# Fifteen short transfers between the q weights and the first K tile of a decode block

## The chip, the cores and the metric

The kernel runs on one core of a Trainium2 chip. The core has five engines that run their own instruction streams: TensorE (PE, matrix products), VectorE (DVE), ScalarE (ACT), GpSimd (POOL) and SyncE (SP). SP computes nothing here; it issues transfers. The transfers themselves are carried out by 16 DMA engines, which fill the on-chip memory (SBUF, 128 partitions) from the device memory (HBM). The metric is the device time of one execution in microseconds. Three executions of the kernel before took 377.62, 377.65 and 378.11 us; the median is 377.65 us.

## The reference, cut to what matters

One decode step of a transformer block for four sequences: layer norm, attention over the last 4096 positions of a cache with 32 query heads and 16 key heads of width 128, output projection, residual, layer norm, a gated feed-forward with ReLU on the gate, residual.

```python
def _A_ref(x, k_cache, v_cache, wq, wo):        # x: (4, 1, 576)
    W = min(4096, max(256, Sk // 4))            # 4096 of 16384 positions
    q = (x @ wq).reshape(B, Sq, Hq, Dh) ...
    k = jnp.repeat(k_cache[:, :, Sk - W:, :], rep, axis=1)
    v = jnp.repeat(v_cache[:, :, Sk - W:, :], rep, axis=1)
    p = _softmax(einsum("bhqd,bhkd->bhqk", q, k) * Dh ** -0.5)
    return einsum("bhqk,bhkd->bhqd", p, v) ... @ wo
def _B_ref(x, W_gate, W_up, W_down):
    gate, up = x @ W_gate, x @ W_up
    return ((gate * (gate > 0)) * up) @ W_down
h  = x + _A_ref(_layernorm(x), A_k_cache, A_v_cache, A_wq, A_wo)
h2 = h + _B_ref(_layernorm(h), B_W_gate, B_W_up, B_W_down)
```

Everything is bfloat16. Nearly all bytes are the K and V windows (16 tiles of 4 MB each) and the five weight matrices, about 160 MB, and each is used once.

## The kernel before, in words

The kernel is written against a small recorder, the class `Prog`. Calls of `P.op` and `P.dma` append one operation to the list of one engine, with the names of the operations that it depends on; `emit` (L71) then writes each list out in that order and puts a semaphore wait ahead of an operation where a dependency lies on another engine or on a transfer. So the order on each engine is the order in which the Python code records, and nothing is moved afterwards. A transfer raises its semaphore by 16 when all of it has landed.

All large transfers are recorded for SP, in one long list near the top of the kernel (L251 to L286). They land in `arena`, a buffer of 81,920 bfloat16 columns: two areas of 8,192 columns (`QWW`) and then a ring of four slots of 16,384 columns (`NSLOT`, `TILE`). `place` (L216) records a transfer into a stretch of `arena` and makes it wait for the last readers of that stretch. `add_kv` (L235) takes the next slot of the ring for a K or V tile: four heads of one sequence, 128 rows of 32 KB, issued at L242. The list begins with

- L251: the last 64 rows of the q weights into `pp` (128 rows of 4 KB),
- L255: the other 512 rows of the q weights into one ring slot (128 rows of 32 KB, 4 MB),
- L242: K tiles 0, 1 and 2 into the other three slots. None of these five waits for anything.
- L242: K tile 3, which takes the slot of the q weights and so waits for the q products (`QMM`, L381 and L34) that read them; then K and V tiles in turn, each waiting for the products that read the tile before it in its slot,
- L266 to L284: the output projection's weights, gate, up, and the down weights in five pieces.

The transfer of `x` (four rows of 1,152 bytes, L337) is issued from ACT, and SP's last transfer writes the output (L710). After it SP waits for its landing (an operation without an instruction, whose wait is made at L110).

What uses the data: PE makes q from the q weights (L381), ACT spreads q into `arena` (L415). For each K tile DVE transposes 32x32 blocks in place (L424) and PE makes the scores (L448 and, with the weights held, `mm_same`, L34). Every four K tiles the softmax of a sequence follows (L453 to L490), and PE multiplies by the V tiles (L509, L34), whose results DVE and ACT select (L519 to L526). The end is the output projection (L617), a layer norm on small tiles (L620 to L647), gate and up (L666), and the down projection (L690, with the last row's weights loaded at L699), copied out at L708 and L709.

Of the kernel before, what the change touches and what calls it, by code (L numbers as in the profile page):

```python
# [9 lines left out]
BF16 = mybir.dt.bfloat16  # L10
# [110 lines left out]
def bass_sequential_preLN__sliding_block_cached__glu_gated_reglu__decode_kernel(  # L121
# [12 lines left out]
    with ExitStack() as es:  # L134
        cnt = [0]

        def sb(name, shape, dt):
            return es.enter_context(nc.sbuf_tensor("sb_" + name, shape, dt))

        P = Prog()  # L140
# [5 lines left out]

        PPW = 6144
        AW = 2 * QWW + NSLOT * TILE
        arena = sb("arena", [128, AW], BF16)
        pp = sb("pp", [128, PPW], BF16)  # L150
        ident_b = sb("ident_b", [128, 128], BF16)
# [64 lines left out]
        def place(name, off, size, reader, make, key=None):  # L216
            deps = []
            for blk in range(off // 64, (off + size) // 64):
                r = owner.get(blk)
                if r is not None and r not in deps:  # L220
                    deps.append(r)
                owner[blk] = reader
            semk = key or "d_" + "_".join(str(v) for v in name)
            P.dma("sync", ("L",) + name, make, semk, deps)
            land[name] = off
# [3 lines left out]
        def ring_slot():  # L229
            s = ring[0] % NSLOT  # L230
            ring[0] += 1
            return s


        def add_kv(kind, g):  # L235
            b, qd = divmod(g, 4)
            s = ring_slot()
            off = slot0 + s * TILE
            cache = A_k_cache if kind == "K" else A_v_cache
            src = cache[b, 4 * qd:4 * qd + 4, SK - WIN:SK, :].rearrange("a (p t) d -> p a (t d)", p=32)  # L240
            place((kind, g), off, TILE, ("QK", g) if kind == "K" else ("PV", g),
                  lambda e: e.dma_start(out=arena[:, off:off + TILE], in_=src), key=f"slot{s}")  # L242


        def main_rows(W):
            return W[0:512, :].rearrange("(p r) n -> p (r n)", r=4)

        def last_rows(W):
# [5 lines left out]
        place(("wq", 0), wq_off, TILE, "QMM",  # L254
              lambda e: e.dma_start(out=arena[:, wq_off:wq_off + TILE], in_=main_rows(A_wq)), key=f"slot{s}")  # L255
        for g in range(NTILE):
            add_kv("K", g)
            if g >= 4:
                add_kv("V", g - 4)
# [3 lines left out]
        for g in range(NTILE - 4, NTILE):  # L263
# [5 lines left out]
        place(("gu", 0, 4), off, F, ("GU", 1, 4), lambda e, off=off: e.dma_start(  # L269
            out=bass.AP(tensor=arena, offset=off, ap=[[2 * AW, 64], [1, F]]), in_=B_W_gate[512:576, :]))  # L270
        P.dma("sync", ("L", "gu", 1, 4), lambda e, off=off: e.dma_start(
            out=bass.AP(tensor=arena, offset=AW + off, ap=[[2 * AW, 64], [1, F]]), in_=B_W_up[512:576, :]), "d_gu_1_4")
        gu_off[(0, 4)] = gu_off[(1, 4)] = off
# [8 lines left out]
        for r0, r1 in zip(WD_ROWS, WD_ROWS[1:]):  # L282
            place(("wd", r0), wd_off + r0 * D, (r1 - r0) * D, ("DOWN", 1),
                  lambda e, r0=r0, r1=r1: e.dma_start(  # L284
                      out=arena[:, wd_off + r0 * D:wd_off + r1 * D],
                      in_=B_W_down.rearrange("(p r) n -> p (r n)", p=128)[:, r0 * D:r1 * D]))  # L286
# [18 lines left out]
                                                in_=c_qm[:, :, :].rearrange("p q (h j) -> p q h j", j=4),  # L305
# [4 lines left out]
                                                in_=to_v[:, :, :].rearrange("p n (k a) -> p n k a", a=4),  # L310
# [14 lines left out]
        for sg in range(2):  # L325
            pool(f"c_toq{sg + 1}", lambda e, sg=sg: e.affine_select(
                out=toq[:, :, :, :], in_=toq[:, :, :, :],
# [84 lines left out]
        def put_q():  # L412
            for i in range(4):
                for q in range(2):
                    act("QW", lambda e, i=i, q=q: e.copy(  # L415
                        out=bass.AP(tensor=arena, offset=32 * i * AW + 2 * i + q, ap=[[AW, 32], [512, 16], [136, 4], [32, 4]]),
                        in_=bass.AP(tensor=q_keep, offset=q, ap=[[512, 32], [32, 16], [8, 4], [2, 4]])),
# [9 lines left out]
        def pe_qk(g):  # L427
            b, qd = divmod(g, 4)
            for cb in range(4):
                for w in range(2):  # L430
                    for a in range(4):
# [8 lines left out]
                        lhsT = arena[:, b * 2048 + cb * 512 + g % 4 * 128 + a * 32:][:, 0:32]  # L440
                        rhs = bass.AP(tensor=arena, offset=off, ap=[[AW, 128], [128, 64], [16, 4], [4, 2]])
                        out_ = bank[w][32 * a:32 * a + 32, :]
# [98 lines left out]
        def finish_o():  # L541
            for q in range(4):
                for qd in range(4):
# [17 lines left out]
                                              in_=bass.AP(tensor=e8, offset=0, ap=[[8, 128], [0, 4], [1, 8]])), ["c_e8", "c_selc0"])  # L561
# [47 lines left out]
        for a in range(8):  # L609
            for n in range(2):  # L610
                for j in range(4):
# [4 lines left out]
                    else:  # L616
# [6 lines left out]
                                             in_=bass.AP(tensor=psb, offset=512 + 224, ap=[[4096, 128], [1, 64], [0, 2]])), ["part1"])  # L623
# [54 lines left out]
        for i in range(2):  # L678
            dve(("HHT", i), lambda e, i=i: e.transpose(
                out=hhT[:, 576 * i:576 * i + 576].rearrange("p (r q) -> p r q", q=32),  # L680
                in_=bass.AP(tensor=pp, offset=3712 + 18 * i, ap=[[PPW, 128], [1, 18], [36, 32]])), [("HH", m) for m in range(3)])
# [26 lines left out]
        dve("OUT0", lambda e: e.tensor_copy(out=out_sb[:, 0:272], in_=bank[0][0:32, 0:272]), [("DOWN", 0)])  # L708
        act("OUT1", lambda e: e.copy(out=out_sb[:, 272:576], in_=bank[1][32:64, 0:304]), [("DOWN", 1)])  # L709
        P.dma("sync", "O", lambda e: e.dma_start(out=out.rearrange("b s d -> (b s) d"), in_=out_sb[0:B, :]), "d_out", ["OUT1", "OUT0"])  # L710
        P.op("sync", None, None, ["O"])
        P.emit(nc, es)


# [26 lines left out]
```

## Time and profile before

| what | value |
|---|---|
| median of three executions | 377.65 us (377.62 to 378.11) |
| the profiled execution | 378.22 us |
| its span, first to last instruction | 377.0 us |
| DMA: bytes, mean rate | 159.74 MB, 424 GB/s |
| share of the 16 DMA engines' time on SP's queue (q1) | 98.7% |
| PE, DVE, ACT busy | 57%, 61%, 14% of the span |
| granted PE clock, mean | 0.796 |

The profile has a page, and views that a reader can ask for: a timeline of instructions, a chain of waits that ended last, sums of waits, and DMA queues. "SPq" stands for SP issuing a transfer: that duration is the issuing only, and the transfer goes on afterwards. "us to landing" runs from the issue to the moment at which the semaphore has its full count. Under the views lie the trace's records of single DMA packets (start, duration, bytes, queue; the number of the DMA engine is not kept) and of single landings: each transfer over 16 DMA engines leaves 16 landings, one for each engine.

### The profile page before, as it was taken

The page shows a single profiled execution, that of the slowest core. Times are in us where ns is not written, and L with a number is a line of the kernel's source. Part 1 is how long each engine was busy: PE and PEld are TensorE (multiplying, and loading weights), DVE is VectorE, ACT ScalarE, POOL GpSimd, SP SyncE. Part 2 cuts the span into 40 slices and gives each one's busy share as a digit, 9 for nine tenths or more (in the row PEclk, how much of TensorE's full clock was granted, in tenths as well). Part 3 has the DMA queues.
Part 4 walks back from the last instruction along what each step waited for, and adds up shares of the span by engine and source line. Part 5 has one row for each costly group of instructions (what it writes and reads, how often), then busy time and mean ns, then how long its engine had stood idle before and what let it go on. Part 6 is the DMA issues. An engine that isn't in the chain of part 4 may idle for free.

```text
span 377.0 us, 2556 instructions
## 1 busy us (share of the span) xinstructions
PE 213.8 (57%) x1462; PEld 39.9 (11%) x694; DVE 228.8 (61%) x164; ACT 53.7 (14%) x84; POOL 10.5 (3%) x29
## 2 busy tenths in 40 slices
PE   0404443239919091749282844664655787886658
PEld 0000000001001010001010100110000101002316
DVE  4088878779292969584847778665749433333240
ACT  3093000211000114010101140101010411112010
POOL 8200000000000000000000000000000000000000
PEclk9966666659969788696877786989695968998686
DMA  8999999999999999999999999999999999999996
GB/s 334 445 445 428 405 445 442 396 442 445 398 435 445 442 433 403 442 445 435 407 436 445 435 414 431 441 438 431 417 442 438 426 417 442 418 433 437 427 414 256
DMA packets 6378, 159.74 MB, mean 424 GB/s; under 512 B 728, under 2 KB 864, under 8 KB 1248
## 3 DMA queue, kind: packets, MB, share of 16 engines
q1 hardware_dynamic: 6360, 159.59, 98.7%
q8 instruction: 8, 0.13, 0.1%
q14 instruction: 2, 0.02, 0.0%
q10 hardware_dynamic: 8, 0.00, 0.0%
HBM read 159.58 MB, written 0.00 MB: 423 GB/s over the span
## 4 chain that ended last, share of the span: by engine, by line
DMA 60%; PE 20%; DVE 18%; SPq 1%; issue 0%; ACT 0%
DMA sb_arena<-in_A_k_cache_dram 53%; DVE sb_arena L424 16%; PE psb L34 11%; DMA sb_arena<-in_B_W_down_dram 7%; PE psb L448 4%; PE psb L509 3%; PE psb L690 2%; DVE sb_o_tmp L522 1%; DVE sb_pp L487 1%; SPq L242 0%; PE psb L475 0%; SPq L255 0%; ACT sb_out_sb L709 0%; SPq L251 0%; DVE sb_f L534 0%
## 5 line engine op out<-in xcount | busy, mean ns | idle before, releaser
L424 DVE STREAM_TRANSPOSE sb_arena<-sb_arena 128x8192 f32<-128x8192 f32 (+1 forms) x19 | 139.9, 7366 | 67.3 <-DMA sb_arena<-in_A_k_cache_dram 67.3
L448 PE MATMUL psb<-sb_arena 128*32 128x512 bf16 x256 | 42.8, 633 | 119.6 <-DVE sb_arena L424 119.5
L34 PE MATMUL psb<-sb_arena,sb_pp 128*128 128x512 bf16 (+1 forms) x386 | 108.7, 392 | 0.0
L509 PE MATMUL psb<-sb_arena,sb_pp 128*128 128x512 bf16 x128 | 50.8, 397 | 8.9 <-DVE sb_o_tmp L522 8.9
L519 ACT COPY sb_o_tmp<-psb 32x512 f32<-32x512 f32 x32 | 18.5, 577 | 182.0 <-PE psb L34 181.7
L34 PE MATMUL psb<-sb_arena 128*32 128x512 bf16 x256 | 43.6, 642 | 0.0
L522 DVE TENSOR_TENSOR sb_o_tmp<-psb,sb_fm 32x512 f32<-32x512 f32 x32 | 21.7, 678 | 18.6 <-PE psb L34 18.1
L448 PEld LDWEIGHTS psb<-sb_arena 128*32 128x32 bf16 x256 | 9.5, 119 | 161.9 <-DVE sb_arena L424 132.7
L509 PEld LDWEIGHTS psb<-sb_arena,sb_pp 128*128 128x128 bf16 x128 | 12.8, 100 | 116.6 <-issue 116.6
L526 DVE TENSOR_REDUCE sb_o_sel<-sb_o_tmp 128x128 f32<-128x512 f32 x16 | 17.7, 1106 | 0.5
L467 ACT ACTIVATE sb_pp<-psb,sb_hx 128x1024 bf16<-128x1024 f32 x4 | 4.5, 1113 | 79.4 <-DVE sb_hx L464 79.4
L487 DVE TENSOR_TENSOR sb_pp<-psb,sb_m 128x1024 bf16<-128x1024 f32 x8 | 9.3, 1206 | 4.9 <-PE psb L475 4.9
L482 ACT ACTIVATE sb_pp<-psb,sb_m 128x512 bf16<-128x512 f32 x16 | 9.7, 690 | 14.9 <-PE psb L475 14.9
L525 DVE TENSOR_TENSOR sb_o_tmp<-sb_o_tmp,sb_fm 64x512 f32<-64x512 f32 x16 | 11.0, 689 | 0.5
L415 ACT COPY sb_arena<-sb_q_keep 32x256 bf16<-32x256 bf16 x8 | 9.7, 1451 | 0.1
L690 PE MATMUL psb<-sb_arena,sb_pp 128*32 128x272 bf16 (+1 forms) x70 | 7.6, 396 | 3.7 <-DMA sb_arena<-in_B_W_down_dram 3.7
L401 DVE CAST sb_pp<-psb 128x512 bf16<-128x512 f32 x1 | 2.4, 2427 | 10.5 <-PE psb L381 10.5
L470 DVE STREAM_TRANSPOSE sb_pp<-sb_pp 128x1024 bf16<-128x1024 bf16 x4 | 5.0, 1245 | 5.1 <-ACT sb_pp L467 5.1
L475 PE MATMUL psb<-sb_pp,sb_to_v 128*32 128x256 bf16 x64 | 4.3, 400 | 6.3 <-DVE sb_pp L470 6.3
L690 PEld LDWEIGHTS psb<-sb_arena,sb_pp 128*32 128x32 bf16 x70 | 6.0, 131 | 5.1 <-DMA sb_arena<-in_B_W_down_dram 3.9
L34 PE MATMUL psb<-sb_arena,sb_hnT 128*32 128x384 bf16 x80 | 6.5, 407 | 0.0
L381 PE MATMUL psb<-sb_arena,sb_xnT 128*32 128x512 bf16 x16 | 2.6, 628 | 6.3 <-DMA sb_arena<-in_A_wq_dram 6.3
(120 smaller groups left out, 81.5 us busy)
## 6 DMA issues: line engine op xcount, KB each, us to landing
sb_arena<-in_A_k_cache_dram SPq DMA_DIRECT2D x16, 4096.0 KB, 26.3
sb_arena<-in_A_v_cache_dram SPq DMA_DIRECT2D x16, 4096.0 KB, 28.5
sb_arena<-in_A_wo_dram SPq DMA_DIRECT2D x1, 4608.0 KB, 24.8
sb_arena<-in_B_W_gate_dram SPq DMA_DIRECT2D x1, 4608.0 KB, 27.7
sb_arena<-in_A_wq_dram SPq DMA_DIRECT2D x1, 4096.0 KB, 12.7
sb_arena<-in_B_W_up_dram SPq DMA_DIRECT2D x1, 3456.0 KB, 27.3
sb_arena<-in_B_W_down_dram SPq DMA_DIRECT2D x1, 2160.0 KB, 26.5
sb_arena<-in_B_W_down_dram SPq DMA_DIRECT2D x1, 1440.0 KB, 29.6
```

The lines of the kernel that those rows point to most:

```text
L34: return e.add_instruction(mybir.InstMatmult(name=e.bass.get_next_instruction_name(), engine=mybir.EngineType.PE, ins=[e.lower_ap(rhs), e. ...
L415: act("QW", lambda e, i=i, q=q: e.copy(out=bass.AP(tensor=arena, offset=32 * i * AW + 2 * i + q, ap=[[AW, 32], [512, 16], [136, 4], [32, 4]]),
L424: dve(("TRA", g), lambda e: e.transpose(out=dst, in_=src), [("L", "K", g)] if lo == 0 else [])
L448: fn = lambda e, out_=out_, lhsT=lhsT, rhs=rhs, start=start, stop=stop: e.matmul(out_, lhsT=lhsT, rhs=rhs, start=start, stop=stop, skip_gr ...
L482: act(("EV", b, 0), lambda e, a=a: e.activation(out=bass.AP(tensor=pp, offset=2 * a, ap=[[PPW, 128], [8, 2], [32, 128], [1, 2]]), in_=bank ...
L487: dve(("EV", b, 1), lambda e, n=n: e.tensor_tensor(out=bass.AP(tensor=pp, offset=16 + 8 * n, ap=[[PPW, 128], [32, 128], [2, 4], [1, 2]]), ...
L509: fn = lambda e, lhsT=lhsT, rhs=rhs, k=k, j=j: e.matmul(bank[2 + j], lhsT=lhsT, rhs=rhs, start=(k == 0), stop=(k == 7), skip_group_check=True)
L519: act(("OSC", g), lambda e, j=j: e.copy(out=o_tmp[32 * j:32 * j + 32, 0:512], in_=bank[2 + j][32 * j:32 * j + 32, :]), [("PV", g), ("OSEL" ...
L522: dve(("OSD", g), lambda e, j=j: e.tensor_tensor(out=ot(32 * j, 32), in0=bank[2 + j][32 * j:32 * j + 32, :].rearrange("p (t d) -> p t d", ...
L525: dve(("OS", g), lambda e: e.tensor_tensor(out=ot(64, 64), in0=ot(64, 64), in1=fmb(64, 64), op=ALU.mult), [("OSC", g)])
L526: dve(("OSEL", g), lambda e: e.tensor_reduce(out=o_sel[:, qd, b, :], in_=o_tmp[:, 0:512].rearrange("p (t d) -> p d t", d=DH), axis=AX.X, o ...
L690: return lambda e: e.matmul(out_, lhsT=lhsT, rhs=w[:, lo:hi], start=start, stop=stop, skip_group_check=True)
```

## The change

A new SBUF tile `mark`, 128 by 1024 bfloat16 (2 KB in each partition), is allocated ahead of `arena`. Ahead of K tile 0, and so behind the two q-weight transfers, SP issues 15 transfers. Transfer k (1 to 15) copies k rows of 40 + k elements (82 to 110 bytes each) from the top left corner of the q weights into `mark`, at column 64 k, the rows four partitions apart. That is 120 rows and some 12 KB together. Nothing reads `mark`. All 15 count on one semaphore, and the wait at the end of SP's list also waits for the last of them.

```diff
@@ -146,6 +146,7 @@
         AW = 2 * QWW + NSLOT * TILE
+        mark = sb("mark", [128, 1024], BF16)
         arena = sb("arena", [128, AW], BF16)
@@ -254,6 +255,10 @@
         for g in range(NTILE):
+            if g == 0:
+                for k in range(1, 16):
+                    P.dma("sync", ("L", "mark", k), lambda e, k=k: e.dma_start(
+                        out=bass.AP(tensor=mark, offset=64 * k, ap=[[4 * 1024, k], [1, 40 + k]]), in_=A_wq[0:k, 0:40 + k]), "d_mark")
             add_kv("K", g)
@@ -708,7 +713,7 @@
-        P.op("sync", None, None, ["O"])
+        P.op("sync", None, None, ["O", ("L", "mark", 15)])
         P.emit(nc, es)
```

In the program that is built, the instructions of PE, DVE, ACT and POOL stand in the same order as before; SP has 15 transfers more (53 for 38 rows of its list).

## The prediction

> **What bounds the kernel now.** I read the page first (slices, DMA queues, chain), then SP's timeline and waits, the start of the chain of waits, and the tail.
>
> ```profile
> span 377.0 us, 2556 instructions
> ...
> DMA  8999999999999999999999999999999999999996
> ...
> q1 hardware_dynamic: 6360, 159.59, 98.7%
> ...
> q10 hardware_dynamic: 8, 0.00, 0.0%
> ...
> DMA 60%; PE 20%; DVE 18%; SPq 1%; issue 0%; ACT 0%
> ...
> sb_arena<-in_A_k_cache_dram SPq DMA_DIRECT2D x16, 4096.0 KB, 26.3
> ...
> sb_arena<-in_A_wq_dram SPq DMA_DIRECT2D x1, 4096.0 KB, 12.7
> ```
>
> The DMA engines work in every slice, and SP's queue alone fills 98.7% of their time. The chain's 60% for DMA understates it: by the landing records a 4 MB tile follows the last one every 9.71 us, yet a K tile takes 26.3 us from issue to landing, so more than two tiles always stand queued ahead. PE and DVE run in that stream's shadow. The end comes when the stream runs out, so two things move it: a hole in the stream, or work added to the DMA engine that finishes last.
>
> Start of the chain of waits (start, duration, what):
>
> ```profile
> 0.80 0.40 SPq L251
> ...
> 1.25 0.41 SPq L255
> 1.66 0.05 issue
> 1.71 0.62 SPq L242
> 2.33 0.04 issue
> 2.37 0.68 SPq L242
> ```
>
> SP's timeline late in the run, and its waits:
>
> ```profile
> 313.16 0.49 SPq L269 DMA_DIRECT2D sb_arena<-in_B_W_gate_dram  x1
> 313.69 0.60 SPq L271 DMA_DIRECT2D sb_arena<-in_B_W_up_dram  x1
> ...
> 340.90 2.23 SPq L284 DMA_DIRECT2D sb_arena<-in_B_W_down_dram  x5
> 375.64 0.33 SPq L710 DMA_DIRECT2D out_dram<-sb_out_sb  x1
> ```
>
> ```profile
> SPq L242 <- PE psb L381: 14.7, 1, 14.7
> ...
> SPq L110 <- DMA out_dram<-sb_out_sb: 1.0, 1, 1.0
> ```
>
> An issue costs SP 0.33 to 0.68 us, and 0.04 to 0.05 us lie between two. After K2, SP idles 14.7 us for the q products. That idle time and the 4 MB of q weights are the cover for new issues.
>
> Tail of the timeline:
>
> ```profile
> 373.72 1.32 PE L690 MATMUL psb<-sb_arena,sb_pp 128*32 128x304 bf16 x15
> ...
> 374.76 0.42 PE L34 MATMUL psb<-sb_arena,sb_pp 128*32 128x272 bf16 x2
> ```
>
> The last product starts at 374.76 us, 0.04 us behind the last landing of the down weights (374.72 in the landing records). A later stream moves the end one for one.
>
> **The change part by part.**
>
> *1. SP's fifteen issues.* They stand ahead of K0, K1 and K2, so these are issued later; K3 waits for the q products until 18.47 us anyway. A deadline decides. By the packet records the q weights' rows leave the DMA engines between 13.18 us (first engine done) and 13.58 us (last); K0's rows now start 6 ns behind. The first issue (0.80) has its first packet at 1.83, so issue to packet is 1.03 us; K0's issue is itself 0.2 us longer than that one. K0 must start by about 13.18 - 1.03 - 0.2 = 11.95 us. It started at 1.71, so the fifteen may take 10.24 us, 0.68 us each with the gap.
>
> What one costs is not shown: no issue before has so few rows, partition steps and 14 like it ahead. Low end: the output's four rows, 0.33 + 0.04, fifteen times 5.6 us, K0 at 7.3, hidden. The two transfers whose rows step over partitions, as the marks' do, are L269 and L271: 0.49 and, straight behind, 0.60. Back-to-back K issues are 0.62 and 0.68. In both pairs the follower is dearer, and here fourteen follow. I take the dearest row, 0.68 + 0.04 = 0.72: 15 x 0.72 = 10.8 us, K0 starts at 12.5, **0.55 us** late. That hole is in all 16 DMA engines. The nearest row (0.49 + 0.04: 8.0 us, K0 at 9.7) leaves 2.2 us to spare; I take the upper one because the cheap rows have no queue of issues ahead. Every further 0.1 us per issue costs 1.5 us, so the upper end is open; at 1.0 us each K0 is 4.8 us late.
>
> *2. The DMA engines' share.* Four rows of `x` left 8 packets on q10: four of 1,152 bytes and four of 4 bytes, which raise the semaphore, so each row went to a DMA engine of its own. So one DMA engine gets a row from all fifteen, the next from fourteen, and one from none. [...]
> Packet records price them: 1,152 bytes 51 ns, 80 bytes 9 ns, 4 bytes 9 ns. The first DMA engine gets 15 x (12 + 9) = 0.3 us (12 ns for 82 to 110 bytes is an estimate between the two), at most 15 x (51 + 9) = 0.9 us. With a hole of 0.55 us it lies in the hole, as the marks stand ahead of K0 in the queue. Without a hole it counts only if that engine finishes last: landings of one tile spread 0.38 us at first and 1.8 us at the end, so an early engine would absorb it. Taken at nothing; 0 to 0.9 us if the hole is gone.
>
> *3. K tiles 0 to 2 later.* DVE's first transpose waits for K0's landing (about 23.7 us) and moves with the hole, which is already counted. Each later tile moves by as much, in the stream and in the slots' releases alike. K3 still has more than 20 us of queue ahead at 18.47.
>
> *4. The last wait.* Behind the output's landing SP has one more wait, long satisfied: one gap, 0.04 us, at least 0.
>
> *5. `mark`'s 2 KB.* It shifts `arena`. No row depends on an address; nothing, within the spread of the three runs (0.49 us) either way.
>
> Sum on the profiled execution: 378.22 + 0.55 + 0.04 = 378.8. It stands 0.57 above the median, so the median after is **378.2 us**, +0.15%. A change within 0.2% (0.76 us) is about what a measurement of this kernel can't tell from none.
>
> **The rivals.**
>
> *A, the hole is long (slower).* The same place; it decides from 0.73 us per issue with the gap, 0.05 above the 0.68 us at which the hole opens. For it: small row counts, a state the trace hasn't; 20 transfers in the queue at once where it shows about eight at 343 us, and if SP is held until the q weights land (13.95 us), K0's packets come at 15.2, 2 us late. Against it: the nearest rows are under 0.60, and the output's four rows cost no more than a full 128 (0.33). At 0.85 + 0.04 us K0 starts at 15.1, 3.1 us late: **380.8 us**.
>
> *B, completions one at a time (slower).* The output's last 4-byte packet is at 376.60 and its landing at 376.93, 0.33 us later. If the first DMA engine may not start the next mark before the last one is confirmed, it loses 15 x 0.33 = 5.0 us, less the 1.2 us that it may have been ahead of the last one: **381.5 us**. Against it: behind each tile's 4-byte packet the next tile's row starts at once. From 0.13 us per mark it would show ((0.76 + 1.2) / 15).
> [...]
>
> *C, hidden whole.* The nearest rows hold: **377.7 us**.
>
> *D, faster.* At 46.3 us a 16 KB instruction packet of 1.03 us falls on one DMA engine, and the landing spread jumps from 0.37 to 1.63 us; it hits an engine that was already behind. Should the marks shift who is behind, 0.4 us can go, **377.3**; all of the spread (1.8) is the bound, 375.9. Against it: the change only adds work.
>
> **How the numbers follow.** Forecast (K0 0 to 0.75 us late) 0.24; C 0.21; A 0.38; B 0.10; D 0.07. A's chance is spread from 0.8 us to over 5, so the densest stretch, the forecast and C together, keeps the predicted time: 378.2, own range 377.5 to 378.4. The forecast and C end within 0.2% save 0.03 (the small packets unabsorbed), A and B slower, D half within: slower 0.51, same 0.45, faster 0.04; as a run may differ for reasons no row shows, I move 0.04 from same to faster: 0.08. The range runs from 377.3 (D's likelier half) to 381.5 (most of A, half of B), which leaves out about 0.15.
>
> **What would show it.** Right: the fifteen issues at 0.6 to 0.72 us each in SP's timeline, K0's issue at 11 to 12.6 us, its landing up to 0.6 us later, all later landings by the same. Step 1 is wrong if K0's issue is past 13 us (A) or below 10 (C). Step 2 is wrong if one DMA engine's landings trail by over a microsecond from K0 on while SP was in time (B). A changed landing spread without either points to D. The prediction falls if a mark costs SP clearly more than any issue seen so far.

## The result and the profile after

The changed kernel takes **379.44 us** (median of five executions, 379.38 to 379.54), the kernel before beside it 377.65 us. The ratio is 1.0045 with a 95% interval of 1.0030 to 1.0059, so it is slower, by 1.79 us between the medians. The profiled execution took 379.44 us, against 378.22 us for the profiled one of before.

The page after (spans, rate in 40 slices, SP's queue, the chain by engine, one group of transfers):

```profile
span 378.2 us, 2556 instructions
...
GB/s 333 379 399 444 444 438 440 402 437 444 435 430 409 441 442 430 426 423 440 437 432 419 430 444 433 425 423 437 440 426 426 428 437 440 424 423 440 417 417 263
...
q1 hardware_dynamic: 6600, 159.60, 98.4%
...
DMA 52%; PE 23%; DVE 20%; SPq 3%; issue 1%; ACT 0%
...
sb_arena<-in_A_wq_dram SPq DMA_DIRECT2D x1, 4096.0 KB, 12.9
```

The rates before, from the same place of its page:

```profile
GB/s 334 445 445 428 405 445 442 396 442 445 398 435 445 442 433 403 442 445 435 407 436 445 435 414 431 441 438 431 417 442 438 426 417 442 418 433 437 427 414 256
```

SP's queue has 240 packets more (120 rows and 120 completions) and fills 98.4% of the DMA engines' time where it filled 98.7%: less of a longer span. The loss is at the front: the second and third slices moved 379 and 399 GB/s where both had 445, and from the fourth on (444, 444, 438) the stream is back at its old rates. And SPq has gone from 1% to 3% of the chain. The chain itself shows where; its start (start, duration, what):

```profile
1.25 0.41 SPq L256
1.66 0.04 issue
1.70 0.32 SPq L260
2.02 0.04 issue
2.06 0.72 SPq L260
...
12.01 0.80 SPq L260
12.81 0.04 issue
12.85 12.82 DMA sb_arena<-in_A_k_cache_dram
```

In this kernel L252 and L256 issue the q weights, L260 the fifteen transfers, L243 the K and V tiles. The chain now begins with SP's fifteen issues, one after the other, and only then reaches K0: they have become what K0 waits for. SP's timeline gives the sum:

```profile
0.80 0.39 SPq L252 DMA_DIRECT2D sb_pp<-in_A_wq_dram  x1
1.25 0.41 SPq L256 DMA_DIRECT2D sb_arena<-in_A_wq_dram  x1
1.70 11.11 SPq L260 DMA_DIRECT2D sb_mark<-in_A_wq_dram  x15
12.85 26.10 SPq L243 DMA_DIRECT2D sb_arena<-in_A_k_cache_dram  x5
```

Fifteen issues took 11.11 us and K0 was issued at 12.85 us instead of 1.71. The DMA engines by the microsecond (length, busy time of PE, PEld, DVE, ACT and POOL, granted clock, DMA share, GB/s):

```profile
12.00:13.00 1.00, 0.00 (x0) 0.00 (x0) 0.00 (x0) 0.00 (x0) 0.18 (x1) 1.00 0.91 393
13.00:14.00 1.00, 0.00 (x0) 0.00 (x0) 0.00 (x0) 0.00 (x0) 0.00 (x0) 1.00 0.17 13
14.00:15.00 1.00, 0.85 (x12) 0.28 (x8) 0.00 (x0) 0.00 (x0) 0.00 (x0) 1.00 1.31 393
15.00:16.00 1.00, 1.00 (x16) 0.16 (x4) 0.00 (x0) 0.00 (x0) 0.00 (x0) 1.00 0.33 131
```

The same stretch before:

```profile
13.00:14.00 1.00, 0.03 (x4) 0.03 (x4) 0.00 (x0) 0.00 (x0) 0.00 (x0) 1.00 1.23 524
14.00:15.00 1.00, 1.00 (x12) 0.24 (x8) 0.00 (x0) 0.00 (x0) 0.00 (x0) 1.00 1.23 524
```

A packet is booked whole in the microsecond in which it starts, so a share can exceed 1. Between 13 and 14 us the stream stands: 13 GB/s instead of 524. What does move there is the small rows. By the packet records they run from 13.16 to 13.89 us, 11 to 13 ns each. One string holds a row of each of the fifteen transfers, about 15 ns from one to the next (13.67 to 13.89 us); beside it stand one of transfers 2 to 15 (from 13.62) and one of 3 to 15 (from 13.64), so the rows stack up on the same DMA engines. Then the engines are idle until K0's first rows start at 14.26 to 15.25 us. Those rows take 1.23 to 2.19 us each (1.21 to 1.29 before) and all end between 16.26 and 16.49, where they ended between 14.40 and 14.80. The landing records add that the small transfers were not finished when their packets were: their completions arrive from 13.76 to 16.79 us. That is 3.03 us for fifteen transfers, 0.2 us for each; which DMA engine a completion belongs to is not kept.

From there the delay is carried along. All DMA engines are late by nearly as much: K0's first landing comes 1.70 us later (25.08 against 23.38) and its last 1.96 (25.68 against 23.72). By the last landing of each tile it is K0 +1.96 us, K1 +1.95, K2 +1.92, K3 +1.54, and +1.27 at the last of the down weights (375.98 against 374.72). The step at K3 is where the first 16 KB instruction packet falls on one DMA engine (at 49.05 us, 1.03 us long). That engine then lands K3 last, 1.0 us behind the others here and 1.2 us before. Which engine it hit the records do not keep; that it had more time to spare here than before would explain the smaller number, but is not shown. SP's slack ahead of K3 went the way of the train of issues, from 14.7 to 3.9 us, and still covered K3:

```profile
SPq L243 <- PE psb L386: 3.9, 1, 3.9
```

The end follows the stream as it did before. The last product starts 0.04 us behind the last landing:

```profile
376.02 0.34 PE L34 MATMUL psb<-sb_arena,sb_pp 128*32 128x272 bf16 x2
...
376.86 0.29 SPq L715 DMA_DIRECT2D out_dram<-sb_out_sb  x1
```

### The profile page after: what moved, and what is told of

It is laid out like the page before. It is cut to its first block, busy times and chain, and to the rows that moved or that the text cites. A ratio compares the mean times of both kernels' runs of the same rounds, so it can differ in the third digit from the quotient of the medians.

```text
span 378.2 us, 2556 instructions
## 1 busy us (share of the span) xinstructions
PE 210.3 (56%) x1447; PEld 39.0 (10%) x694; DVE 228.4 (60%) x164; ACT 53.7 (14%) x84; POOL 10.5 (3%) x29
## 3 DMA queue, kind: packets, MB, share of 16 engines
q1 hardware_dynamic: 6600, 159.60, 98.4%
## 4 chain that ended last, share of the span: by engine, by line
DMA 52%; PE 23%; DVE 20%; SPq 3%; issue 1%; ACT 0%
DMA sb_arena<-in_A_k_cache_dram 45%; DVE sb_arena L429 16%; PE psb L34 13%; DMA sb_arena<-in_B_W_down_dram 7%; PE psb L453 4%; PE psb L514 3%; SPq L260 3%; PE psb L695 2%; DVE sb_o_tmp L527 1%; DVE sb_pp L492 1%; PE psb L480 1%; DVE sb_pp L475 0%; DVE sb_hx L458 0%; ACT sb_pp L472 0%; SPq L256 0%
## 5 line engine op out<-in xcount | busy, mean ns | idle before, releaser
L34 PE MATMUL psb<-sb_arena,sb_pp 128*128 128x512 bf16 x384 | 107.9, 390 | 3.0 <-issue 2.9
L453 PE MATMUL psb<-sb_arena 128*32 128x512 bf16 x256 | 42.2, 630 | 120.6 <-DVE sb_arena L429 120.6
L514 PE MATMUL psb<-sb_arena,sb_pp 128*128 128x512 bf16 x115 | 44.9, 390 | 8.9 <-DVE sb_o_tmp L527 8.9
L34 PE MATMUL psb<-sb_arena 128*32 128x512 bf16 x256 | 43.2, 642 | 0.0
L531 DVE TENSOR_REDUCE sb_o_sel<-sb_o_tmp 128x128 f32<-128x512 f32 x16 | 17.7, 1108 | 0.5
```

The costliest lines, as they stand in the source:

```text
L34: return e.add_instruction(mybir.InstMatmult(name=e.bass.get_next_instruction_name(), engine=mybir.EngineType.PE, ins=[e.lower_ap(rhs), e. ...
L453: fn = lambda e, out_=out_, lhsT=lhsT, rhs=rhs, start=start, stop=stop: e.matmul(out_, lhsT=lhsT, rhs=rhs, start=start, stop=stop, skip_gr ...
L514: fn = lambda e, lhsT=lhsT, rhs=rhs, k=k, j=j: e.matmul(bank[2 + j], lhsT=lhsT, rhs=rhs, start=(k == 0), stop=(k == 7), skip_group_check=True)
L531: dve(("OSEL", g), lambda e: e.tensor_reduce(out=o_sel[:, qd, b, :], in_=o_tmp[:, 0:512].rearrange("p (t d) -> p d t", d=DH), axis=AX.X, o ...
```

## The experiments

The theory that the result suggests: the whole loss is K0's late issue, that is SP's time. The rival: the small rows themselves cost the DMA engines time. Unless a diff says otherwise, an experiment is the kernel before with the lines shown, with the tile `mark` and the last wait of the change. Runs 3 and 10, which have no small transfers, keep the last wait of the kernel before.

**1. The fifteen transfers behind K0's issue, same transfers as in the change.** If SP's time is all, nothing is left of the loss.

```diff
             add_kv("K", g)
+            if g == 0:
+                for k in range(1, 16):
+                    P.dma("sync", ("L", "mark", k), lambda e, k=k: e.dma_start(
...
```

> The fifteen transfers stand behind K0's issue in place of ahead of it; same transfers, same tile, same last wait. Theory 1 (the issues delay K0, and the stream has a hole between the q weights and K0): K0 is issued at 1.7 us again, K1 at about 13.5 us, 9 us before the stream needs it; no hole, K0 lands at about 23.7 us as before the change, time 377.65 us within 0.3. Theory 2 (the transfers themselves cost the DMA engines, or the moved tile or the last wait cost): the time stays near that of the changed kernel, 379.4 us.

```profile
1.71 0.63 SPq L243 DMA_DIRECT2D sb_arena<-in_A_k_cache_dram  x1
2.38 11.44 SPq L261 DMA_DIRECT2D sb_mark<-in_A_wq_dram  x15
13.87 5.31 SPq L243 DMA_DIRECT2D sb_arena<-in_A_k_cache_dram  x3
```

The windows of the same kernel:

```profile
24.00:25.00 1.00, 0.00 (x0) 0.00 (x0) 1.00 (x1) 0.99 (x2) 0.00 (x0) 0.50 0.73 264
25.00:26.00 1.00, 0.00 (x0) 0.00 (x0) 1.00 (x1) 1.00 (x2) 0.00 (x0) 0.50 0.32 132
26.00:27.00 1.00, 0.00 (x0) 0.00 (x0) 1.00 (x1) 0.99 (x2) 0.00 (x0) 0.50 1.28 525
```

380.59 us (379.88 to 380.74), ratio 1.0071 (1.0058 to 1.0085) to 377.73 us of before: slower than the change, and the number of neither theory. There is no hole: K0 is issued at 1.71 us and has landed by 23.92. But the small rows now stand in a running stream, between K0 and K1, and they pass from 22.99 to 26.80 us, not in 0.73 us as in the changed kernel.

The length of a row tells its transfer (80 + 2k bytes). From 22.99 us on, rows of transfers 6 to 15, one of each, follow each other at about 15 ns: one DMA engine passes its ten at once. Not so the engines with the most rows, which come to them later: the last row of each transfer comes 0.11 to 0.40 us behind the last row of the one before, from 23.38 us on. The completions arrive from 23.57 to 27.13 us, 3.57 us for fifteen transfers (0.24 for each). K1's landings lie 3.08 us apart where K0's lay 0.55 apart: twelve come by 34.42 us and four from 36.04 to 36.87. Of each of transfers 12 to 15, too, just four rows come late (from 24.98 us on), so the four are the DMA engines with twelve or more small rows. The spread at the end is still 3.42 us. The others are late as well, if less: no DMA engine ends its first row of K1 before 24.88 us, where in the kernel before all sixteen had by 24.61. Those that start it first, at 23.14 to 23.23, take 1.69 to 1.80 us for it instead of 1.21.

So removing the hole removed nothing; it uncovered a second cost.

**2. Cheaper issues in the old place.** Only the destination changes: rows in neighbouring partitions instead of four apart.

```diff
-  out=bass.AP(tensor=mark, offset=64 * k, ap=[[4 * 1024, k], [1, 40 + k]])
+  out=bass.AP(tensor=mark, offset=64 * k, ap=[[1024, k], [1, 40 + k]])
```

> The fifteen transfers in the same place, with the same rows and bytes, into neighbouring partitions in place of every fourth. If the step over partitions is what makes an issue cost SP 0.64 to 0.80 us, an issue falls to 0.33 to 0.48 us as for the other transfers without a step, K0 is issued at 6.7 to 9 us, in time, and by theory 1 the time is 377.65 us within 0.3. If the small row counts or the train make the cost, issues stay at 0.7 us and the time at 379.4 us. Theory 2 (the transfers on the DMA engines cost) says 379.4 us whatever the issues cost.

```profile
1.70 5.51 SPq L260 DMA_DIRECT2D sb_mark<-in_A_wq_dram  x15
7.25 11.35 SPq L243 DMA_DIRECT2D sb_arena<-in_A_k_cache_dram  x4
```

The train costs 5.5 us instead of 11.1, 0.24 to 0.41 us an issue, and K0 is in the queue at 7.25 us, nearly 6 us before the q weights' rows end. Still it takes 380.27 us (380.04 to 380.43), ratio 1.0066 (1.0053 to 1.0079), 0.8 us more than the change and again the number of neither theory. The fifteen rows of the busiest DMA engine run from 13.7 to 17.7 us, their completions arrive from 13.76 to 18.00 (0.28 us for each transfer), and K0's landings are 3.59 us apart. In the changed kernel the completions took 0.2 us for each as well; but there every DMA engine was waiting for K0 anyway.

**3. The late issue alone.** No small transfers at all; SP waits ahead of K0 for an added memset on GpSimd.

```diff
+            if g == 0:
+                P.op("sync", None, None, ["c_late"])
             add_kv("K", g)
...
+        pool("c_late", lambda e: e.memset(mark[:, 0:512], 0.0))
```

> No small transfers at all: SP waits ahead of K0 for one more fill of 512 columns on POOL, which ends at about 12.7 us, so K0 is issued at nearly the time of the changed kernel (12.85 us). Theory 1: the same hole, K0 lands 1.8 to 2 us later than before the change, time 379.2 to 379.5 us. Theory 2 (the transfers cost, not their place): 377.65 us. In between: the hole is a part of it and the small transfers the rest.

```profile
12.70 5.75 SPq L243 DMA_DIRECT2D sb_arena<-in_A_k_cache_dram  x4
```

The windows of the same kernel:

```profile
13.00:14.00 1.00, 0.00 (x0) 0.00 (x0) 0.00 (x0) 0.00 (x0) 0.00 (x0) 1.00 0.01 0
14.00:15.00 1.00, 0.89 (x12) 0.27 (x8) 0.00 (x0) 0.00 (x0) 0.00 (x0) 1.00 1.67 524
15.00:16.00 1.00, 1.00 (x16) 0.16 (x4) 0.00 (x0) 0.00 (x0) 0.00 (x0) 1.00 0.00 0
```

379.44 us (379.14 to 379.49), ratio 1.0042 (1.0030 to 1.0055): the time of the changed kernel, without a single small transfer. K0 is issued at 12.70 us; its first rows start 1.41 to 2.15 us later and are slow (1.31 to 2.14 us), done at 16.01 to 16.25. So the late issue alone is enough for all that the change costs. That it costs 1.6 us (by the ratio; 1.7 between the medians), where K0 was 0.75 us past the prediction's deadline, is a slower restart than was counted.

**4. The kernel before again.** The same code in the same round of runs.

> The kernel before, unchanged, for a second profile of it. The first profiled execution took 378.22 us, 0.57 above the median, and in it the first 16 KB instruction packet fell on the DMA engine that was already last. If that engine's load is what the 0.57 is, an execution at 377.6 us shows the packet on another engine and a spread of landings that is smaller by about 0.4 us from the fourth tile on; if the placement is the same in both, the 0.57 is something else. Time 377.65 us within 0.3.

377.81 us, ratio 1.0001 (0.9992 to 1.0009). Its profiled execution took 377.82 us and has its last landing at 374.37 us, so the changed kernel's 375.98 is 1.61 us later, and its 379.44 us are 1.62 us more. The 1.27 us of the first comparison were thus short because the first profiled execution of before was a late one, 0.57 us over its median. The place of the instruction packet does not explain it: the packet took the spread from 0.53 to 1.68 us here too. The cause stays open.

**5. One transfer with the same small pieces.** Behind K0 again, but 16 rows of 15 pieces each in one transfer: each DMA engine gets 15 pieces of 110 bytes and one completion.

```diff
+                P.dma("sync", ("L", "mark", 15), lambda e: e.dma_start(
+                    out=bass.AP(tensor=mark, offset=0, ap=[[1024, 16], [64, 15], [1, 55]]),
+                    in_=A_wq[0:16, 0:960].rearrange("p (c n) -> p c n", n=64)[:, :, 0:55]), "d_mark")
```

> In the place behind K0: one transfer of 16 rows of 15 pieces of 110 bytes, so every one of the 16 DMA engines gets 15 small packets, as the first did, but one completion in place of fifteen. If the completions, one after the other, are what costs a DMA engine 0.2 to 0.3 us per small transfer in the running stream, the time falls to 377.7 to 378.0 us. If the short packets cost that themselves, all 16 DMA engines now lose up to 15 x 0.28 = 4 us: 380.5 to 382 us.

378.49 us (378.26 to 378.70), ratio 1.0017 (1.0008 to 1.0027): a cost of 0.7 us, with twice the small rows of run 1, where it was 2.9. That is between the two expectations, much nearer to the first. The pieces pass in 0.77 us (22.88 to 23.65); the 0.7 us stand in the rows behind them, since K1's first rows take 1.49 to 1.95 us instead of 1.21. What is dear is the number of transfers, and so of completions, less the number of small rows.

**6. Longer rows.** The fifteen transfers of run 1 with rows of 642 to 670 bytes, each row in a partition of its own.

```diff
-  out=bass.AP(tensor=mark, offset=64 * k, ap=[[4 * 1024, k], [1, 40 + k]]), in_=A_wq[0:k, 0:40 + k]
+  out=bass.AP(tensor=mark, offset=1024 * (k * (k - 1) // 2), ap=[[1024, k], [1, 320 + k]]), in_=A_wq[0:k, 0:320 + k]
```

> In the place behind K0: the same fifteen transfers with rows of 642 to 670 bytes in place of 82 to 110, into a partition of its own for each row. If rows this short are slow to write, rows of 640 bytes are not: by bytes 15 x (33 + 9 ns) = 0.6 us on the first DMA engine, time 378 to 378.4 us. If each transfer costs whatever its rows' length, the time stays at 380.3 to 381.0 us.

380.81 us (380.42 to 381.33), ratio 1.0079 (1.0064 to 1.0095). Not the length of the rows, nor their sharing a destination row.

**7. Rows of their own.** As run 1, but each transfer reads other rows and columns of the q weights.

```diff
-  in_=A_wq[0:k, 0:40 + k]
+  in_=A_wq[32 * k:33 * k, 256 * k:256 * k + 40 + k]
```

> The fifteen transfers straight behind K0's issue again, each reading rows and columns of its own of the q weights in place of the same first rows. If the cost (380.6 us there) comes from all of them reading the same few rows of memory, it goes: 377.7 to 378.3 us. If it comes from fifteen transfers back to back on one DMA engine, wherever they read, it stays: 380.2 to 381.0 us, and the first K tile's successor lands with a spread of about 3 us.

380.52 us (380.15 to 380.70), ratio 1.0072 (1.0057 to 1.0087), K1's landings 3.51 us apart. Reading the same few rows is not the cause.

**8. The change with thirteen of its fifteen transfers.**

```diff
-                for k in range(1, 16):
+                for k in range(1, 14):
...
-        P.op("sync", None, None, ["O", ("L", "mark", 15)])
+        P.op("sync", None, None, ["O", ("L", "mark", 13)])
```

> The changed kernel with its first thirteen transfers. K0 is issued at about 11.2 us, in time. If the hole is all that costs there, the time is 377.7 to 378.0 us. If the small transfers cost a DMA engine 0.2 to 0.3 us each as soon as the stream runs on behind them, as behind K0, then up to 13 x 0.28 less some lead: 379.5 to 380.3 us, no less than with fifteen.

```profile
1.71 9.43 SPq L260 DMA_DIRECT2D sb_mark<-in_A_wq_dram  x13
11.19 7.51 SPq L243 DMA_DIRECT2D sb_arena<-in_A_k_cache_dram  x4
```

379.20 us (379.02 to 379.37), ratio 1.0036 (1.0023 to 1.0050): two transfers fewer gain only 0.24 us, though K0 is issued at 11.19 us, 1.66 us earlier. For small rows that cost, 379.5 us or more had been expected. Its first rows end at 15.75 to 16.55, hardly earlier than in the changed kernel. Either 11.19 us is still too late, or the small rows (13.20 to 14.91 us here, more than twice as long as in the changed kernel) now hold K0 up: their completions arrive from 13.77 to 16.43, 0.2 us for each transfer. But here the loss does not sit on the DMA engines with many small rows. K0's landings lie 0.69 us apart, and all are late (24.66 to 25.35, before the change 23.38 to 23.72). Three DMA engines start their first row of K0 at 13.51 to 13.65 us and take 2.77 to 2.90 us for it, so that they end it last. All thirteen rows of transfer 13 start meanwhile (14.52 to 14.90), so these three have none of them.

**9. One transfer behind each K tile.** The same fifteen transfers, the k-th behind the issue of K tile k.

```diff
+            if g:
+                for k in [g]:
+                    P.dma("sync", ("L", "mark", k), lambda e, k=k: e.dma_start(
...
```

> The fifteen transfers one at a time, transfer k behind the issue of K tile k (1 to 15). The same packets, transfers and completions in all, but each alone between 4 MB tiles. If the cost comes from small transfers back to back, the time is 377.7 to 378.0 us. If each costs 0.2 to 0.3 us wherever it stands, the first DMA engine loses up to 4 us: 379.5 to 381 us.

```profile
1.71 1.32 SPq L243 DMA_DIRECT2D sb_arena<-in_A_k_cache_dram  x2
3.07 0.48 SPq L261 DMA_DIRECT2D sb_mark<-in_A_wq_dram  x1
3.60 0.54 SPq L243 DMA_DIRECT2D sb_arena<-in_A_k_cache_dram  x1
4.19 0.73 SPq L261 DMA_DIRECT2D sb_mark<-in_A_wq_dram  x1
```

377.74 us (377.54 to 377.92), ratio 0.9999 (0.9989 to 1.0008). The issues cost SP as much as ever, but it has the time, and a single small row between two large ones costs its DMA engine nothing that can be measured. The tile `mark` and the last wait cost nothing either.

**10. A shorter wait.** Run 3's edit with a GpSimd operation that ends earlier, and neither small transfers nor the tile `mark`: K0 is issued when run 8 issued it.

```diff
+            if g == 0:
+                P.op("sync", None, None, ["c_toq2"])
             add_kv("K", g)
```

> The kernel before with one wait of SP's ahead of K0 and without the fifteen transfers; the wait is for an earlier GpSimd operation than in the first wait run (it ends at about 11.1 us), so K0 should be issued at about 11.15 us, where thirteen transfers put it. The prediction's deadline of 11.95 us (issue to first packet 1.23 us): K0 is in time, 377.6 to 378.0 us, and what the run with thirteen transfers lost (+1.4 us) came from the small packets. An emptied or nearly empty queue restarts slowly (3.3 us from issue to the first row's end, as in the first wait run): K0's first rows end at about 14.5 to 15.8 us instead of 14.4 to 14.8, and the time is 378.3 to 379.0 us.

```profile
1.25 0.41 SPq L255 DMA_DIRECT2D sb_arena<-in_A_wq_dram  x1
11.14 8.01 SPq L242 DMA_DIRECT2D sb_arena<-in_A_k_cache_dram  x4
```

The windows of the same kernel:

```profile
13.00:14.00 1.00, 0.00 (x0) 0.00 (x0) 0.00 (x0) 0.00 (x0) 0.00 (x0) 1.00 1.29 524
```

377.97 us (377.72 to 378.16), ratio 1.0005 (0.9996 to 1.0014). K0 at 11.14 us is in time: 524 GB/s from 13 to 14 us, first rows done at 14.47 to 14.92. So run 8's 1.4 us came from its thirteen small transfers, which stood ahead of a K0 already issued. How they hold up DMA engines that have no row of the last of them, no run shows. And the deadline lies between 11.14 us (nothing lost) and 12.70 us (1.6 us lost): the 1.56 us between these two issues cost 1.4 to 1.6 us, so almost all of them were past it.

**11. Five transfers.** Run 1 with only transfers 11 to 15.

```diff
-                for k in range(1, 16):
+                for k in range(11, 16):
```

> The last five of the fifteen transfers (11 to 15 rows), straight behind K0's issue, so that no hole opens and each of the first eleven DMA engines gets five small rows. If each small transfer in a row costs the engine 0.2 to 0.3 us from the first one on (fifteen cost 2.6 to 2.9 us of the whole time), five take 1.0 to 1.4 us off eleven engines, less the 0.5 us or so by which the slowest of them may be ahead: 378.3 to 378.9 us. If only a long train is dear, or what is dear is the wide range of transfers open at once, 377.6 to 378.0 us, as with one transfer behind each K tile.

377.89 us (377.78 to 378.52), ratio 1.0005 (0.9995 to 1.0015). Nearly all rows of a DMA engine follow each other at about 15 ns. The completions do take 1.4 us in all (23.56 to 24.95), but the next large rows are under way meanwhile. This train of five costs nothing that can be measured.

**12. Sixteen rows in each.** Run 1 with 16 rows in every transfer, so that no DMA engine moves large rows while another stands at small ones.

```diff
-  ap=[[4 * 1024, k], [1, 40 + k]]), in_=A_wq[0:k, 0:40 + k]
+  ap=[[4 * 1024, 16], [1, 40 + k]]), in_=A_wq[0:16, 0:40 + k]
```

> Fifteen transfers straight behind K0's issue, as in the run that cost most, but each of sixteen rows, so that every one of the 16 DMA engines gets fifteen small rows (240 in all in place of 120) and none runs ahead with 32 KB rows while the others stand at small ones. If a small transfer is dear only because the other engines are moving large rows meanwhile, all fifteen pass in 15 to 50 ns each, 0.25 to 0.8 us in all, as ahead of K0 in the changed kernel: 377.9 to 378.7 us, with a spread at the next landing of under 1 us. If each transfer beyond the first few in a row costs its engine 0.2 to 0.3 us whatever the others do, all sixteen engines lose 2.5 us or more: 380.2 to 381.5 us, and no spread.

```profile
22.00:23.00 1.00, 0.00 (x0) 0.00 (x0) 0.40 (x3) 1.00 (x2) 0.00 (x0) 0.50 0.54 229
23.00:24.00 1.00, 0.00 (x0) 0.00 (x0) 0.18 (x1) 1.00 (x1) 0.00 (x0) 0.50 0.10 7
24.00:25.00 1.00, 0.00 (x0) 0.00 (x0) 1.00 (x1) 0.99 (x3) 0.00 (x0) 0.50 0.07 6
25.00:26.00 1.00, 0.00 (x0) 0.00 (x0) 1.00 (x1) 1.00 (x2) 0.00 (x0) 0.50 1.26 502
```

380.64 us (380.43 to 380.82), ratio 1.0072 (1.0055 to 1.0088). Now the whole stream stands, for two microseconds at 6 to 7 GB/s: the first rows of transfers 1 to 3 start within 0.03 us (23.11 to 23.14), those of transfers 4 to 15 0.06 to 0.41 us apart (23.28 to 25.42), and K1's first rows start at 25.4 to 26.0 us. The 240 completions arrive at an even pace from 23.60 to 26.65 us, 0.2 us for each sixteen. The cost does not need neighbours that move large rows. And 240 completions take as long as the 120 of the changed kernel (3.05 and 3.03 us): the time goes with the number of transfers, not with the number of completions.

Together: two costs, each enough for most of the loss, and they do not add. K0 issued late costs 1.6 us (run 3). A train of thirteen to fifteen small transfers ahead of tiles already issued costs 1.4 to 3 us (runs 1, 2, 6, 7, 8, 12). The completions of such a train take 0.2 to 0.28 us for each transfer; this pace is in the landing records of the changed kernel too, where 3.03 us of completions (to 16.79) lay beside the wait for K0 and its slow first rows (to 16.49). That the two ended together would explain why neither undoing the late issue (run 2) nor leaving out the rows (run 3) gains anything by itself.

The length of the rows (6), the memory they read (7) and the load from other DMA engines (12) are excluded as the cause; one completion for each DMA engine (5), trains of five (11) and single transfers (9) are cheap. That the pace of completions holds the DMA engine up fits the four late engines of run 1 and all sixteen of run 12, but it is argued: no run changed the pace alone, and all transfers of a run count on one semaphore, which no run changed either. It does not cover everything. In run 8 the slowest first rows are on DMA engines with the fewest small rows, and in run 1 those whose small rows were over first had a slow row of K1 behind them. How far an engine may run ahead of its completions stays open as well: three rows or so in run 12, ten in run 1, all fifteen in the changed kernel.

No version tried beats the kernel before.

## Why the prediction was right and wrong

The time lies within the range and on the side given the larger chance. But it is 1.24 us above the predicted 378.2, and outside the forecast's own range (377.5 to 378.4): what happened is rival A's case, a long hole in the place named. The range held because it was drawn wide enough for A and for half of B; the number came from a sum that was too small in one term.

- **Step 1, the issues: nearly right.** The dearest row of before, 0.68 + 0.04 us, stood for them; the fifteen averaged 0.743 us from one start to the next (the issues themselves 0.32 for the single row, then 0.64 to 0.80). K0 was issued at 12.85 us, predicted 12.5. The reason given, that followers in a queue are dearer, was wrong: run 2 has the same queue at 0.24 to 0.41 us. With the same rows and bytes, the partition step is what makes the issue dear.
- **Step 1, the deadline: the term that failed.** "K0 must start by about 13.18 - 1.03 - 0.2 = 11.95 us" took the issue-to-packet time of the very first transfer, and took for granted that the first row then runs at full speed. In run 3, without any small transfer, 1.41 to 2.15 us passed from issue to packet and the first rows took up to 2.14 us in place of 1.21. From K0's issue to its first rows' end it was 3.3 to 3.6 us in run 3, and 3.4 to 3.6 in the changed kernel, not 1.23 + 1.21 = 2.44. That is some 1.0 us, and with the 0.35 us of the later issue the predicted 0.55 becomes 1.9, which is K0's measured delay of 1.96 us.
  Counted from the end of SP's issue, the first packet of the very first transfer came after 0.63 us (1.03 us from the start of an issue of 0.40); behind the emptied queue of run 3 it took longer (1.41 to 2.15 from the start of an issue of 0.62, so 0.79 to 1.53).
- **Step 2, the DMA engines' share: right here, wrong in its bound.** The small rows lie in the hole, 11 to 13 ns each where 12 was estimated, and run 3 has the same time without them. That one DMA engine gets a row of all fifteen was assumed, as no row of before shows where the rows of several small transfers go; the changed kernel's packet records show it, and the fifteen pass in 0.22 us where 0.3 was summed. But "0 to 0.9 us if the hole is gone" was far too low: with K0 issued in time they cost 1.4 to 2.9 us (runs 1, 2 and 8). The packets' durations were priced; the pace of the completions and the slow large rows behind the small ones were not.
- **Steps 3 to 5: right.** K0 to K2 moved together (by 1.96, 1.95 and 1.92 us), K3 kept cover (3.9 us), the wait and the tile cost nothing measurable (run 9, ratio 0.9999).
- **Rival A** had the right place and size but its mechanism only in part: its threshold of 0.73 us per issue was met by 0.743, yet at that price it would have given only about 0.9 us. The rest is the slow restart.
- **Rival B** saw completions one at a time rightly, at 0.2 us for each where it took 0.33. With the measured 3.03 us its own sum gives 3.03 - 1.2 = 1.8 us, which is by chance the measured loss; so the time alone can't tell it from A. The landings say more: B makes the DMA engines with many rows late, 3.1 to 4.0 us of spread as in runs 1, 2, 6 and 7, while in the changed kernel all are late by 1.70 to 1.96 us. That alone does not decide, since run 8 has all late by nearly as much with K0 in time; what decides is run 3, which has the same time without a small transfer. Once K0 is in time, the train costs as much or more, but B's mechanism is only argued there. Its objection, that behind a tile's completion the next tile's row starts at once, holds for single transfers and for five in a row (runs 9, 11), not for a longer train.
  Which transfer a completion belongs to is not in the records.
- **C** would have needed issues of 0.63 us with the gap or less, as run 10's K0 at 11.14 us shows, and then, as run 2 shows, it would not have been hidden either. **D** did not happen: nothing was faster.
- **What would show it**: "K0's issue at 11 to 12.6 us, its landing up to 0.6 us later", and wrong "if K0's issue is past 13 us". It was 12.85, between the two, with a landing 1.96 us later, a case the list had not.

## What to carry to other kernels

In a kernel like this one, which lives on one stream of transfers, the issuing engine's time is free only as long as the next large transfer is in the queue well before the queue runs dry: here 11.14 us was in time and 12.70 us was not, for a stream that ran dry at 13.2. A deadline should be counted to the end of the first row, not to its first packet, and against a queue that is about to be empty: in run 3 that was 3.3 to 3.6 us from K0's issue, where 2.44 had been counted. Small transfers cost least here one by one between large ones (nothing measurable, run 9) or as one transfer (0.7 us, run 5); the trains of thirteen to fifteen were paid either by the issuer (1.8 us, the change) or by the DMA engines (1.4 to 3 us, runs 1, 2, 6, 7, 8 and 12), and moving them from the one to the other was no gain.

## What the runs showed of the hardware

- An issue's cost on SP went with the step between the destination's partitions: for the same two to fifteen rows, 0.64 to 0.80 us with rows four partitions apart (change), 0.24 to 0.41 us with neighbouring ones (run 2). Sixteen rows four apart mostly take 0.59 us (run 12), less than fifteen.
- Completions of thirteen to fifteen small transfers in a row take 0.2 us for each transfer (the changed kernel, runs 8 and 12), 0.24 to 0.28 us in runs 1 and 2, while the packets of 82 to 110 bytes take 11 to 13 ns (the changed kernel). The packets' time alone does not show what these transfers cost.
- The stream that had run dry restarted slowly: the first 32 KB rows took 1.31 to 2.14 us instead of 1.21 (run 3), with no small transfer in the queue. Large rows behind a train of small ones were slow too in two runs (up to 2.90 us in run 8, 1.80 in run 1), but not in run 12 (1.21).
- The first 16 KB instruction packet among the rows took 1.03 us on its DMA engine, and the row behind it 1.68 us instead of 1.21 (the kernel before and the changed kernel, 46.3 and 49.1 us). From there the landings of one tile lay 1.6 us apart where they had been 0.4 to 0.6 apart, and at the end still 1.83 and 1.86.
